# Attention and mixture of experts on one core: the last stores behind the first expert's gather, and four smaller moves beside it

## The chip, the cores and the metric

One core of a Trainium2 chip runs the whole kernel. The metric is the device time of one execution in microseconds. Three runs of the kernel before gave 411.78, 412.25 and 407.70 us; the median is 411.78. One more execution was profiled. The engines named here are TensorE (PE, with its weight loads PEld), VectorE (DVE), ScalarE (ACT), GpSimd (POOL) and SyncE (SP); SP and POOL hand transfers to the DMA engines.

## What is computed

```python
scores = scale * np.matmul(q, k.transpose(0, 1, 3, 2))          # 8 batches, 8 heads, 576 tokens, 64 wide
attn = softmax(np.where(masks, scores, -1e9))                   # heads 0-3 local (32 wide), 4-7 strided by 32
x = np.matmul(attn, v)  ->  (4608, 512)                          # tokens of batch b are rows 576*b ...
out = x.copy()
do_compute = x @ w_skip > 0
e_idx = np.argmax(xc @ w_gate, axis=1)                          # xc = x[do_compute]; one expert of 8 per token
for e in range(8):
    h = np.maximum(xc[mask_e] @ w1[e], 0.0)                     # 512 -> 1024
    y[mask_e] = gate_w[mask_e, None] * (h @ w2[e])              # 1024 -> 512
out[do_compute] = xc + y
```

All numbers are float32. A matmul with a weight is made of three, with each operand split into a rounded part and its remainder (xh and xl, w1h and w1l, w2h and w2l, hh and hl).

## The kernel before

**Attention** (to about 163 us of the profile). A unit is (b, pr): batch b, and pr 0 and 1 for the two parts of the local heads, 2 and 3 for those of the strided ones; 32 units run in turn (loop at L921). For each, qk (L195) makes the scores two units ahead, DVE adds the mask and takes the row maximum mx, POOL subtracts it (L234, into sm or frame; DVE takes part of it in batch 0), tex (L239) turns the result and takes exp, pv (L268) multiplies by V, and xpose (L328) turns the output x. A batch's x goes to DRAM with SP's stores (jobs_out, L313): kind 0 for the local half, 3 transfers, kind 1 for the strided half, 6 transfers in packets of 512 bytes.

**Routing.** score (L373), route1 (L390) and route2 (L439) find each token's expert and its slot; scat (L471) writes a row of the table in DRAM for 128 tokens at a time, an indirect DMA issued by POOL. Groups of one or two batches are routed together; the last three groups are batches 5, 6 and 7, with five scatters each.

**The first expert** ("e") is picked from the counts of batches 0 to 3, and 288 of its tokens, all from batches 0 to 5, are taken before the rest is known. In unit (7,1) POOL reads their table rows (rows, L638; tile tab, 96 partitions by 3), in unit (7,2) it gathers their x back from DRAM (gather, L690; tile xg, three indirect DMAs, L695). After the last unit, xturn (L706) transposes xg on TensorE (L715), ACT rounds it to xh (L717), DVE takes the remainder xl (L718). ffn1a (L752) makes the first two hidden blocks: sixteen matmuls with xh (L760), then eight with xl (L764); hout (L730) makes hh on ACT and hl on DVE. ffn1 (L737) makes hidden blocks 3 to 8, ffn2 the output.

**Weights** come in eight pieces of 512 KB per expert, w1 as pieces 1 to 4 and w2 as 5 to 8 (indices j = 0 to 7 in the code). wdma (L594) fetches a piece into one of three raw buffers, wcast (L605) rounds it on ACT, wrest (L615) subtracts on DVE and frees the buffer. For the first expert the lists CASTS, RESTS and FETCH (L43 to L45) say behind which unit a step stands; pieces 6 and 7 are made to wait for the gather (taken).

**The other experts.** TURN gives their order, by size. Behind the first expert's second matmuls come its overflow tokens ("l", 128 of them) and the experts' tokens r; their table rows are read by POOL and SP, and their gathers wait for all stores and scatters.

The order on each engine is that of the code: manual_schedule keeps it for the engines listed, and an engine runs its queue in that order, each instruction waiting for its semaphores. SP's transfers stand at the hand() calls of the loop.

## Time and profile before

| | us |
|---|---|
| median of three runs | 411.78 |
| profiled execution, its time | 412.99 |
| its span on the core | 411.2 |
| TensorE busy | 383.1 (93%) |
| DVE busy | 271.7 (66%) |
| POOL busy | 209.4 (51%) |
| ACT busy | 194.7 (47%) |
| granted clock, mean of the core | 0.981 |

The profiled execution's time is its span and 1.8 us around it. TensorE is busy nearly all of the span, so the time is read from the places where it waits and where its granted clock is below 1. A timeline row gives the start, the duration, the operation with its tiles, how many were merged, and in brackets the idle time before it with what ended it. A window gives busy times within a stretch.

### The profile page before, as it was taken

To read this page: it belongs to the slowest core of one execution; us is meant where nothing else is said; L and a number is where in the kernel's file an instruction comes from. 1 tells how busy PE (TensorE), PEld (TensorE's weight loads), DVE (VectorE), ACT (ScalarE), POOL (GpSimd) and SP (SyncE) were. 2 spreads that over 40 slices of the span, in tenths; PEclk is the share of its full clock that TensorE was granted. 3 is DMA by queue.
4 is the path that set the end of the run, shared out by engine and by line. 5 is a ranking of instruction groups with operands and counts; after the bars stand their busy time and mean duration, and the time that the engine had idled before them with its cause. 6 is when DMAs were issued, how large, how long until landed. Compare 5 with 4: busy or idle time off the path is not lost. (4 is left out here: it accounts for less than half of the span.)

```text
span 411.2 us, 12396 instructions
## 1 busy us (share of the span) xinstructions
PE 383.1 (93%) x4967; PEld 349.2 (85%) x4968; DVE 271.7 (66%) x526; ACT 194.7 (47%) x372; POOL 209.4 (51%) x296
## 2 busy tenths in 40 slices
PE   6889998989989977799999999999999999999993
PEld 3778887778767766689989999999999999998983
DVE  3767769656886886474268667756757767588640
ACT  1456554637362844152444364554444554555520
POOL 3353425772678686567017577383474473641101
PEclk9899999999998999699999999999999999999999
DMA  7999899999899846608439778697586587685801
GB/s 257 370 337 286 268 288 297 285 274 314 266 233 268 247 135 167 185 4 272 140 104 257 199 221 247 171 250 222 200 208 210 179 241 226 187 260 128 286 8 50
DMA packets 49554, 89.91 MB, mean 219 GB/s; under 512 B 8742, under 2 KB 25518, under 8 KB 49486
## 3 DMA queue, kind: packets, MB, share of 16 engines
q1 hardware_dynamic: 41261, 75.32, 61.3%
q0 software_dynamic: 8224, 13.70, 11.3%
q8 instruction: 41, 0.67, 0.7%
q14 instruction: 28, 0.22, 0.2%
HBM read 70.35 MB, written 15.30 MB: 208 GB/s over the span
## 5 line engine op out<-in xcount | busy, mean ns | idle before, releaser
L721 PE MATMUL S<-xh,w1h 128*128 128x324 f32 (+4 forms) x248 | 75.8, 305 | 0.8 <-DVE hl L734 0.8
L722 PE MATMUL S<-xl,w1h 128*128 128x324 f32 (+4 forms) x248 | 74.1, 299 | 0.0
L723 PE MATMUL S<-xh,w1l 128*128 128x324 f32 (+4 forms) x248 | 74.1, 299 | 0.0
L808 POOL DMA_INDIRECT out_dram<-ot,tab x23 | 27.1, 1176 | 85.6 <-DVE ot L802 51.3
L658 POOL DMA_DIRECT2D xq<-xg x96 | 52.6, 568 | 24.7 <-DVE xt L673 16.6
L617 DVE TENSOR_TENSOR w1l<-raw,w1h 128x1024 fp32r<-128x1024 f32 x32 | 39.0, 1227 | 27.1 <-ACT w1h L612 25.0
L733 ACT ACTIVATE hh<-S 128x324 fp32r<-128x324 f32 (+4 forms) x64 | 26.7, 418 | 52.3 <-PE S L723 42.9
L617 DVE TENSOR_TENSOR w2l<-raw,w2h 128x1024 fp32r<-128x1024 f32 x32 | 39.2, 1224 | 15.5 <-ACT w2h L612 15.4
L721 PEld LDWEIGHTS S<-xh,w1h 128*128 128x128 f32 x248 | 46.8, 189 | 1.2 <-DVE hl L734 1.1
L722 PEld LDWEIGHTS S<-xl,w1h 128*128 128x128 f32 x248 | 46.8, 189 | 0.1
L723 PEld LDWEIGHTS S<-xh,w1l 128*128 128x128 f32 x248 | 46.8, 189 | 0.0
L472 POOL DMA_INDIRECT table<-pay,rdi x38 | 38.8, 1021 | 10.3 <-issue 7.1
L234 POOL TENSOR_TENSOR sm<-sm,mx 128x384 f32<-128x384 f32 (+1 forms) x30 | 27.9, 941 | 31.0 <-PE T L254 13.9
L205 PE MATMUL S<-kt,qt 64*64 64x54 f32 (+1 forms) x1280 | 33.0, 241 | 9.8 <-DVE sm L223 3.5
L205 PEld LDWEIGHTS S<-kt,qt 64*64 64x64 f32 x1280 | 26.9, 139 | 16.0 <-issue 8.6
L734 DVE SCALAR_TENSOR_TENSOR hl<-S,hh 128x324 fp32r<-128x324 f32 (+4 forms) x64 | 29.3, 461 | 12.0 <-ACT hh L733 11.8
L612 ACT CAST w2h<-raw 128x1024 fp32r<-128x1024 f32 x32 | 33.4, 1043 | 5.5 <-DMA raw<-in_w_dram 5.5
L612 ACT CAST w1h<-raw 128x1024 fp32r<-128x1024 f32 x32 | 33.4, 1053 | 4.0 <-DMA raw<-in_w_dram 4.0
L234 POOL TENSOR_TENSOR frame<-sm,mx 128x324 f32<-128x324 f32 (+1 forms) x32 | 22.8, 725 | 18.5 <-DVE mx L229 18.4
L695 POOL DMA_INDIRECT xg<-out_dram,tab x23 | 26.3, 1145 | 11.3 <-issue 6.1
L262 ACT ACTIVATE ptl<-T 96x512 f32<-96x512 f32 (+1 forms) x40 | 19.5, 548 | 23.9 <-PE T L254 23.6
L311 DVE TENSOR_TENSOR x<-PV,rc 128x384 f32<-128x384 f32 (+1 forms) x64 | 29.5, 502 | 1.1
(181 smaller groups left out, 940.9 us busy)
## 6 DMA issues: line engine op xcount, KB each, us to landing
raw<-in_w_dram SPq DMA_DIRECT2D x64, 512.0 KB
vt<-in_vs_dram SPq DMA_DIRECT2D x16, 390.0 KB
qt<-in_qp_dram SPq DMA_DIRECT2D x16, 304.0 KB
kt<-in_kp_dram SPq DMA_DIRECT2D x16, 297.0 KB
kt<-in_kp_dram SPq DMA_DIRECT2D x14, 304.0 KB
vt<-in_vl_dram SPq DMA_DIRECT2D x16, 260.0 KB
out_dram<-x SPq DMA_DIRECT2D x16, 256.0 KB
qt<-in_qp_dram SPq DMA_DIRECT2D x14, 288.0 KB
```

The source lines that it names most:

```text
L205: mark[0] = T.matmul(s[HP * (i ^ j):HP * (i ^ j) + HP, j, (blk - b0) * win:(blk - b0 + 1) * win], lhsT=qt[p, j, blk * nq:blk * nq + HP], r ...
L234: (V if b == kind == 0 and j else G).tensor_tensor(e[:, j], sw[:, j], mx[:, j].unsqueeze(2).broadcast_to([128, b1 - b0, win]), op=ALU.subt ...
L311: V.tensor_tensor(outs[o], num, den, op=ALU.mult)
L472: i = G.indirect_dma_start(out=table, out_offset=bass.IndirectOffsetOnAxis(ap=di[:, t:t + 1], axis=0), in_=pay[:, t, :], in_offset=None, b ...
L612: A.copy(hi, raw)
L617: V.tensor_tensor(lo, raw, hi.bitcast(F32), op=ALU.subtract)
L658: G.dma_start(dst, src)
L721: T.matmul(p, lhsT=a[0], rhs=b[0], start=start, stop=False)
L722: T.matmul(p, lhsT=a[0], rhs=b[1], start=False, stop=False)
L723: T.matmul(p, lhsT=a[1], rhs=b[0], start=False, stop=stop)
L734: V.scalar_tensor_tensor(s["hl"][:, f, :C], p[:, :C], 0.0, s["hh"][:, f, :C].bitcast(F32), op0=ALU.max, op1=ALU.subtract)
L808: i = G.indirect_dma_start(out=out, in_=ot[:P], in_offset=None, bounds_check=NTOK - 1, oob_is_err=False, out_offset=bass.IndirectOffsetOnA ...
```

## The change

Five things move; what is computed stays.

- **SP.** The stores of batch 6's strided half and all of batch 7's, fifteen transfers, move behind the first expert's gather and wait for it, as pieces 5 and 6 do. The stores of batch 6's local half go out in the first two hands of unit (7,0). Piece 4 is fetched at the end of unit (7,0), and pieces 7 and 8 ahead of the reading of the next two experts' rows.
- **POOL.** In unit (7,0) the five scatters of batch 5 take turns with the subtractions; the gather is written in unit (7,1) right behind the row read. The five scatters of batch 6 are cut in three and two, the two behind the sums of the last route1.
- **DVE.** The remainders of pieces 1, 2 and 3 (wrest) move: the first to unit (7,0), the second to (7,1), the third into route2 between its reduction and its slots. The four operations of count move behind the last route1.
- **TensorE.** Nine of the twelve transposes of xg stand ahead of the last route1's five, not six.
- **The last ranks** (route2 of batch 7) stand behind the whole of ffn1a, not between its xh and xl matmuls.

On SP, around the end of attention: raw_2547, raw_2548 and raw_2549 are the three raw buffers; x_2591 and x_2773 are batch 6's halves, x_3005 (x_3009 in the change) and x_3136 (x_3133) batch 7's. Before:

```order
L182 DMA out_dram<-x_2591 128x2x256 x2
L182 DMA out_dram<-x_2591 64x256
L182 DMA out_dram<-x_2773 18x11x128 x2
L182 DMA out_dram<-x_2773 18x10x128
L598 ISA
L598 DMA raw_2547<-in_w_dram 128x1024
L182 DMA out_dram<-x_2773 18x11x128 x2
L182 DMA out_dram<-x_2773 18x10x128
L598 ISA
L598 DMA raw_2548<-in_w_dram 128x1024
L182 DMA out_dram<-x_3005 128x2x256 x2
```

and with the change:

```order
L182 DMA out_dram<-x_2591 128x2x256 x2
L182 DMA out_dram<-x_2591 64x256
L599 ISA
L599 DMA raw_2547<-in_w_dram 128x1024
L599 ISA
L599 DMA raw_2548<-in_w_dram 128x1024
L182 DMA out_dram<-x_2773 18x11x128 x2
L182 DMA out_dram<-x_2773 18x10x128
L182 DMA out_dram<-x_2773 18x11x128 x2
L182 DMA out_dram<-x_2773 18x10x128
L599 ISA
L599 DMA raw_2549<-in_w_dram 128x1024
```

Pieces 4 and 5 (raw_2547, raw_2548) stand ahead of the strided stores of batch 6; piece 5 carries the wait for the gather, and every store behind it stands behind that wait.

On POOL, units (7,0) and (7,1): table is the scatters' target, frame and sm the subtractions' results, tab the rows read, xg the gather. Before:

```order
L234 TENSOR_TENSOR sm_81<-sm_81,mx 128x480 x2
L472 DMA table<-pay_93,rdi 40960x4 x5
L234 TENSOR_TENSOR frame_84<-sm_82,mx 128x6x54 x2
L234 TENSOR_TENSOR frame_85<-sm_83,mx 128x5x54 x2
L640 ISA
L640 DMA tab<-table 96x12
L695 DMA xg_3126<-out_dram,tab 96x512 x3
```

and with the change:

```order
L234 TENSOR_TENSOR sm_81<-sm_81,mx 128x480 x2
L473 DMA table<-pay_93,rdi 40960x4 x2
L234 TENSOR_TENSOR frame_84<-sm_82,mx 128x6x54
L473 DMA table<-pay_93,rdi 40960x4
L234 TENSOR_TENSOR frame_84<-sm_82,mx 128x6x54
L473 DMA table<-pay_93,rdi 40960x4 x2
L234 TENSOR_TENSOR frame_85<-sm_83,mx 128x5x54 x2
L641 ISA
L641 DMA tab<-table 96x12
L696 DMA xg_3049<-out_dram,tab 96x512 x3
```

The same nine instructions stand ahead of the read of tab; the first two subtractions moved ahead of three and two of the scatters, and two follow the last scatter in place of four.

On DVE, from the last route1 (L422 to L425) to the first remainders of the hidden blocks: rdd, rds, rdi and pay are the last ranks and slots, pt, pr, fsel and isel the four operations of count. Before:

```order
L422 TENSOR_TENSOR rohb<-cs,rmw 128x40
L424 TENSOR_REDUCE rrs<-rohb 128x8
L425 TENSOR_TENSOR run_69<-run_70,rrs 128x8
L455 TENSOR_TENSOR rdd<-T,rohb 128x40
L457 TENSOR_REDUCE rds<-rdd 128x5
L459 TENSOR_TENSOR rdi<-rds,rmk 128x5
L460 RECIPROCAL pay_95<-rz 128x5
L734 SCALAR_TENSOR_TENSOR hl<-S,hh 128x288 x2
```

and with the change:

```order
L422 TENSOR_TENSOR rohb<-cs,rmw 128x40
L424 TENSOR_REDUCE rrs<-rohb 128x8
L425 TENSOR_TENSOR run_69<-run_70,rrs 128x8
L516 TENSOR_TENSOR pt_3361<-first,cnt_3263 1x8
L518 TENSOR_REDUCE pr_3363<-pt_3361 1x1
L519 SCALAR_TENSOR_TENSOR fsel<-pr_3363,fsel 1x1
L520 CAST isel<-fsel 1x1
L735 SCALAR_TENSOR_TENSOR hl<-S,hh 128x288 x2
L455 TENSOR_TENSOR rdd<-T,rohb 128x40
```

The two hl stand ahead of the last ranks instead of behind them, and the four operations of count, which stood ahead of the last batch's score copies, are now between route1 and hl.

```diff
--- before.py
+++ after.py
@@ -41,8 +41,8 @@
 PB = 3
 CB = 5
 CASTS = [(6, 3), (7, 0), (7, 1)]
-RESTS = [(7, 1), (7, 2), (7, 3)]
-FETCH = [(6, 0), (6, 1), (6, 3), (7, 2), (7, 3)]
+RESTS = [(7, 0), (7, 1)]
+FETCH = [(6, 0), (6, 1), (6, 3), (7, 0)]
 CE = (96, 3)
 
 CAPS = [(126, 3), (108, 3), (108, 3), (104, 3), (102, 3), (98, 3), (92, 3)]
@@ -177,11 +177,11 @@
             jobs.append((vt[0:LW, LV - 1].rearrange("p h c -> p (h c)"), vh[b]))
         return jobs
 
-    def issue(jobs, behind=None):
+    def issue(jobs, *behind):
         for dst, src in jobs:
             i = nc.sync.dma_start(dst, src).ins
-            if behind is not None:
-                tc.add_manual_dep(i, behind.name, SYNC, reason="a transfer is handed over beside its step")
+            for x in behind:
+                tc.add_manual_dep(i, x.name, SYNC, reason="a transfer is handed over beside or behind its step")
 
     pvp = psum.tile([128, 2, 512], F32, name="PV", tag="PV", bufs=1)
     v2 = [ap.tile([128, LV - 1, 4, 65], F32, name=f"v2{i}") for i in range(2)]
@@ -455,6 +455,7 @@
         V.tensor_tensor(dd, rkv, ohb, op=ALU.mult)
         ds_ = sp("rds", [128, nt])
         V.tensor_reduce(ds_, dd, axis=AX.X, op=ALU.add)
+        yield
         di = sp("rdi", [128, nt], I32)
         V.tensor_tensor(di, ds_, mk, op=ALU.add)
         V.reciprocal(pay[:, :, 2].bitcast(F32), zs)
@@ -930,6 +931,8 @@
             ob = jobs_out(units[n - 4][0], units[n - 4][1] // 2) if n > 3 else [[], []]
             steps = [vj[0:1], vj[1:], ob[0], qk_[0:1], qk_[1:2], qk_[2:3], qk_[3:4], ob[1]]
             steps = [[x for x in y if x is not None] for y in steps]
+            if b == NB - 1:
+                steps = [ob[0], ob[1]] if pr == 0 else []
         if n + LA >= len(units) and "h" not in pool:
             zctx.close()
             pool["h"] = ctx.enter_context(tc.tile_pool(name="hpool", bufs=1, side="right", reuse_waits="tile"))
@@ -965,8 +968,7 @@
         for x in front:
             next(x, 0)
         if b == CB + 2 and pr == 0:
-            while sc_:
-                scat(*sc_.pop(0))
+            scat(*sc_.pop(0))
         run(*rank, *late, *front)
         late = []
         if (b, pr) in RESTS:
@@ -995,8 +997,9 @@
         if n == 1:
             for g in range(len(GROUPS)):
                 payload(g)
-        if sc_ and n + 1 < len(units):
-            scat(*sc_.pop(0))
+        for _ in range(2 if b == CB + 2 and pr == 0 else 1):
+            if sc_ and n + 1 < len(units):
+                scat(*sc_.pop(0))
         if b == PB + 2 and pr == 3:
             e0 = nc.sync.value_load(isel[0:1, 0:1], min_val=0, max_val=NE - 1)
         if b == PB + 2 and pr == 3:
@@ -1009,23 +1012,28 @@
                 assert not sc_
             if pr == 1:
                 rows("e", s0, *CE, eng=G)
-            if pr == 2:
                 gather("e", "e", "e", last=(CB + 1) * S)
     pool_order.close()
     nr = len(GROUPS) - 1
     with tc.manual_schedule(engines={T.engine, A.engine, V.engine, G.engine}):
-        run(pv(*units[-1]), xpose(*units[-2]), route2(ranked, of=CB))
+        r2 = route2(ranked, of=CB)
+        run(pv(*units[-1]), xpose(*units[-2]), islice(r2, tiles(ranked) + 2))
+        wrest("e", 2)
+        run(r2)
+        for _ in range(3):
+            scat(*sc_.pop(0))
+        xe, r1 = xturn("e"), route1(nr)
+        run(xpose(*units[-1]), score(NB - 1), islice(xe, 9))
+        next(r1)
+        run(xe, r1)
+        count(CB)
         while sc_:
             scat(*sc_.pop(0))
-        count(CB)
-        run(xpose(*units[-1]), score(NB - 1), xturn("e", 0, 2))
-        r1 = route1(nr)
-        next(r1)
-        run(xturn("e", 2, 4), r1)
-    for kind in range(2):
-        for part in jobs_out(NB - 1, kind):
-            issue(part)
-    wdma("e", e0, 5, 6, st_["e"]["taken"])
+    with tc.manual_schedule(engines={nc.sync.engine}):
+        for kind in range(2):
+            wdma("e", e0, 4 + kind, 5 + kind, st_["e"]["taken"])
+            for part in jobs_out(NB - 2 + kind, 1 - kind) + jobs_out(NB - 1, 1) * kind:
+                issue(part, *st_["e"]["taken"])
     pctx.close()
     pctx = ExitStack()
     psum, bufs = pctx.enter_context(tc.tile_pool(name="psumT", bufs=1, space=PSUM, reuse_waits="tile")), {"S": 2, "T": 3, "PV": 2, "R": 1}
@@ -1036,22 +1044,23 @@
         x = nc.sync.value_load(order[0:1, n, r:r + 1], min_val=0, max_val=(NE - 1) * (1, ESTR)[n])
         (es, slots)[n][r] = x
 
-    with tc.manual_schedule(engines={T.engine, A.engine, V.engine, G.engine}):
-        run(islice(ga, 8), later(route2, nr), ga)
+    with tc.manual_schedule(engines={T.engine, A.engine, V.engine, G.engine, nc.sync.engine}):
+        run(ga, later(route2, nr))
         while sc_:
             scat(*sc_.pop(0))
         places = sort(NB - 1)
         g = ffn1("e", 2, 6)
         run(islice(g, 4))
         judge, rest = places()
+        wsplit("e", 3, 4)
+        wdma("e", e0, 6, 7)
+        run(islice(g, 4))
+        wsplit("e", 4, 5)
+        wdma("e", e0, 7, 8)
         for r in TURN[:2]:
             load(r, 1)
             assert SMALL[r] == CAPS[r]
             rows(r, slots[r], *CAPS[r])
-        wsplit("e", 3, 4)
-        wdma("e", e0, 6, 7, st_["e"]["taken"])
-        run(islice(g, 4))
-        wsplit("e", 4, 5)
         run(g)
         actx.close()
         pool["b"] = ctx.enter_context(tc.tile_pool(name="bpool", bufs=1, reuse_waits="tile"))
@@ -1069,7 +1078,6 @@
             load(key, 0)
         wdma(key, es[key], j, j + 1)
 
-    ahead(1)
     s0n = G.value_load(isel[0:1, 2:3], min_val=0, max_val=(NE - 1) * ESTR + CE[0] * CE[1])
     rows("l", s0n, CT, 1, eng=G)
     ahead(2)
```

## Rows read from the trace of the kernel before

**Rows 1.** Timeline, TensorE, 150 to 199: start, us, operation, count, [idle before <-releaser]
```profile
154.05 0.76 PE L254 MATMUL T<-cs,frame 128*118 128x128 f32 x5 [1.15 <-POOL frame L234]
...
154.74 0.47 PE L402 MATMUL T<-cs,s9s 9*128 9x9 f32 x5
...
164.06 0.36 PE L715 MATMUL T<-cs,xg 96*128 96x96 f32 x1
...
166.31 0.36 PE L715 MATMUL T<-cs,xg 96*128 96x96 f32 x1 [1.88 <-DMA xg<-out_dram,tab]
...
167.53 0.92 PE L715 MATMUL T<-cs,xg 96*128 96x96 f32 x4 [0.86 <-DMA xg<-out_dram,tab]
...
169.95 0.59 PE L760 MATMUL S<-xh,w1h 128*128 128x288 f32 x1
...
173.69 0.30 PE L760 MATMUL S<-xh,w1l 128*128 128x288 f32 x1
...
174.02 1.31 PE L764 MATMUL S<-xl,w1h 128*128 128x288 f32 x8
...
175.79 0.40 PE L721 MATMUL S<-xh,w1h 128*128 128x288 f32 x1 [0.44 <-DVE hl L734]
...
197.38 0.39 PE L715 MATMUL T<-cs,xg 128*128 128x128 f32 x2
```

**Rows 2.** Windows: us, busy (count) of PE, PEld, DVE, ACT, POOL; granted clock, DMA, GB/s
```profile
158.00:162.00 4.00, 2.26 (x56) 2.02 (x57) 3.04 (x9) 2.07 (x5) 3.26 (x5) 1.00 0.67 158
...
164.00:166.00 2.00, 0.42 (x7) 0.20 (x1) 1.28 (x5) 0.00 (x0) 1.61 (x2) 1.00 0.93 294
...
170.00:172.00 2.00, 2.00 (x10) 2.00 (x9) 1.62 (x6) 0.83 (x3) 0.06 (x1) 0.50 0.91 160
...
178.00:182.00 4.00, 3.65 (x28) 3.41 (x27) 3.75 (x9) 2.78 (x5) 3.27 (x4) 1.00 0.02 1
```

**Rows 3.** Timeline, POOL, 150 to 200
```profile
151.56 3.63 POOL L234 TENSOR_TENSOR frame<-sm,mx 128x324 f32<-128x324 f32 x4
...
157.84 1.04 POOL L695 DMA_INDIRECT xg<-out_dram,tab  x1 [1.53 <-DMA tab<-table]
...
160.47 0.96 POOL L695 DMA_INDIRECT xg<-out_dram,tab  x1 [0.32 <-issue]
...
175.47 1.06 POOL L472 DMA_INDIRECT table<-pay,rdi  x1 [2.04 <-DVE pay L460]
...
180.69 0.98 POOL L472 DMA_INDIRECT table<-pay,rdi  x1 [0.30 <-issue]
...
188.42 1.03 POOL L695 DMA_INDIRECT xg<-out_dram,tab  x1 [0.30 <-issue]
```

**Rows 4.** Issue to landing, us: gathers 157:162, scatters 175:183, gathers 190.6:192
```profile
DMA to landing us min/median/max: 7.0/7.0/7.0
...
DMA to landing us min/median/max: 2.9/2.9/2.9
...
DMA to landing us min/median/max: 7.2/7.2/7.2
```

**Rows 5.** Timeline, SP's queue, 150 to 182
```profile
159.50 0.66 SPq L598 DMA_DIRECT2D raw<-in_w_dram  x1
...
160.20 8.29 SPq L182 DMA_DIRECT2D out_dram<-x  x9
```

**Rows 6.** Timeline, DVE, 149 to 180
```profile
149.48 1.21 DVE L617 TENSOR_TENSOR w1l<-raw,w1h 128x1024 fp32r<-128x1024 f32 x1
...
163.93 0.14 DVE L519 CAST isel<-fsel 1x1 int32<-1x1 f32 x1
...
171.08 0.19 DVE L410 TENSOR_REDUCE rm<-T 128x5 f32<-128x40 f32 x1
...
172.70 0.17 DVE L425 TENSOR_TENSOR run<-run,rrs 128x8 bf16<-128x8 bf16 x1
...
175.28 0.99 DVE L734 SCALAR_TENSOR_TENSOR hl<-S,hh 128x288 fp32r<-128x288 f32 x2
```

## The prediction

> **What bounds the kernel now.** I read the timeline of TensorE first, for its waits, then the windows (busy time and granted clock), then the same minutes of POOL, SP and DVE. From 175.79 on TensorE stops only once more, for 0.35 us, before the tail; up to 154 it stops for little. What can be won lies between. At 164.06 it runs the first transpose of the first expert's tokens (tile xg, L715), then waits 1.88 us and 0.86 us for the rest of the gather [rows 1]. After those waits the granted clock is 0.50, the lower level of 1.2 GHz: it stood at 1.00 while TensorE was busy 2.26 of 4 us (158 to 162), and TensorE was busy only 0.42 of 2 us just before it fell [rows 2]. At that clock the sixteen L760 matmuls stand (173.69 - 169.95) / 15 = 0.249 us apart; 28 matmuls of the same size in 178 to 182 take 3.65 us, 0.130 each [rows 1, 2]. So this place costs twice: waits, then half speed.
>
> Why is the gather late? POOL issues its three parts at 157.84 (when the row table, tab, has landed) to 160.47, and each lands 7.0 us after its issue [rows 3, 4]; 160.47 + 7.0 = 167.5 is where the second wait ends. In those 7 us SP issues a weight piece of 512 KB at 159.50 and nine stores from 160.20 on [rows 5], and the DMA engines are 0.93 busy [rows 2]. Scatters issued in 175 to 183, with DMA at 0.02, land after 2.9 us [rows 4, 2].
>
> **The change, part by part.** I follow one mark: the start of the third hidden block, L721 at 175.79 [rows 1].
>
> *Stores behind the gather.* The order on POOL shows that the gather is not issued sooner: five scatters, four subtractions, the tab read, three gathers, as before; only the turns differ. What moves is SP: it now holds weight piece 5 and the last fifteen stores until the gather has landed. Piece 4 goes out at the end of unit (7,0), as soon as DVE has freed its buffer, long before the gather. So the gather has the DMA engines to itself, and the gain is its landing time alone. No row shows a gather in a quiet stretch. Bounds: 2.9 us, a scatter of 128 short rows in quiet, and 7.0 us, the same gather in traffic. I take the lower bound plus its data: 96 rows of 2 KB are 197 KB, 0.7 us at the 294 GB/s of 164 to 166 [rows 2], so 3.6 us, near the quiet end because the queue will be quiet. The third part then lands at 160.47 + 3.6 = 164.1, not 167.5.
>
> The Trainium skill ("DMA: Bandwidth & Descriptors", Anatomy of one DMA — SWDGE (gpsimd) path) gives about 2.0 us plus bytes at 436 GB/s, an estimate of 2.45 us here; no run here shows that, the 7.0 us of the trace is far from it, and by it the mark below would come 6.1 us sooner in place of 5.8.
>
> *From landing to mark, all at full clock.* Seven transposes at 0.15 (five took 0.76, [rows 1]) end at 165.1. The five L402 transposes take 0.47 to 165.6; the score copies that they need end on DVE by then in either order. The last three L715: 166.0. Then two chains run. TensorE: 16 x 0.130 = 2.1 and eight more in 1.31 [rows 1], to 169.4. Here lies the reason for ranking later: the rank matmuls now stand behind these eight. DVE: the last cast and subtraction of xg (some 0.5 us each, taken from the two hl of 0.99, which are as large) to 167.0; the routing chain, 171.08 to 172.87, 1.8 us; the four count operations on one partition now behind it, 0.14 us each (163.93) and as much again between them or less, 0.7 us in all; the first hl, 0.5 us [rows 6]. That is 170.0, later than TensorE, so DVE sets the mark: **175.79 - 170.0 = 5.8 us** sooner.
>
> *Subtractions in turns.* Each weight remainder is 1.21 us of DVE [rows 6]. The first moves ahead of the mask add of (7,3). That delays TensorE there by 1.21 us at most; it is covered by the 1.15 us that TensorE waited for frame [rows 1], and that wait goes because frame now passes three scatters of 1.3 us ((180.69 - 175.47) / 4, [rows 3]). The third leaves its place between two PV results for one behind the rank sums, worth 1.21 us at most. Neither counts: whether TensorE reaches L715 at 162.8 or 164.06, it has to wait until 164.1. Only a full 1.21 us late and uncovered would show, as 1.2 us. Price 0.
>
> *Scatters in turns.* The same nine instructions stand ahead of the tab read, but only two subtractions instead of four behind the last scatter, for whose landing the read waits. So the last scatter starts two subtractions later, some 1.8 us (four took 3.63, [rows 3]); at its quiet 2.9 us [rows 4] it lands about when the last subtraction ends, at twice that 2.9 us later. I take 0 and keep 2.9 for the range.
>
> *What is late next.* After the mark TensorE is the bound, and everything that it fetches must also come 5.8 us sooner. Two things may not. First, the expert gathers: the overflow tokens' part of 188.42 landed 7.2 us later, at 195.6, and TensorE used it at 197.38 [rows 3, 4, 1]; it will now ask at 191.6. Its chain on POOL starts with the last group's five scatters, 175.47 to 181.67 [rows 3]. They need the last ranks, ready some 3.5 us sooner, but two scatters of the group before (2.6 us) and a register load, which I put at 1 us, now stand between the last routing sums (about 169.5) and them: I get 173.2, 2.3 us sooner, so a landing at 193.3 if it still takes 7.2. That is a wait of up to 1.7 us. It may take less, because pieces 7 and 8 no longer travel beside it: at 5 us no wait is left. I take 0.8. Second, pieces 7 and 8 queue behind all the stores: one and a half batches of 1.18 MB and two pieces, 2.8 MB from 164.2 on; 10 us at 294 GB/s, 18 us at 158 [rows 2]. Landed 3.6 us later and split in 2.3 (cast and subtraction), they are there at 180 to 188; TensorE wants them at about 187. This lies inside the same 0 to 1.7 us.
>
> **Sum.** 5.8 - 0.8 = 5.0 us. The profiled execution took 412.99 us (span 411.2 and 1.8 around it): 408.0. The median of the three runs is 1.2 us lower, so for a median 411.78 - 5.0 = **406.8**.
>
> **Rivals.**
> 1. *The clock still falls.* TensorE still idles about 1.5 us before 164.1. For it: two waits of 1.88 and 0.86 us were enough. Against: 158 to 162 kept 1.00 with as little as 2.26 of 4 us busy [rows 2]. Price: L760 16 x 0.12 = 1.9 us and the transposes at 0.19 to 0.23 (four in 0.92, [rows 1]), 0.7 us; DVE is then no longer last, so the mark comes 3.4 us sooner, and the gathers have time. 408.4. The Trainium skill ("TensorE: Matmul & The Clock Gate", Part 1: The HAM clock gate) says that throttled is the default and activity releases it; the trace agrees in so far as 0.50 came behind the idle stretch and 1.00 came back while TensorE was working (174).
> 2. *The gather lands no sooner:* 7.0 us is its own price, not that of traffic. For it: the expert gathers took 7.2. Against: those too had weights beside them. Then the waits and the clock stay; 0.5 us from the new order of L402. 411.3.
> 3. *The wait is handed on in full* to the expert gathers, with 1.7 us and a little more for the rows fetched by SP: 3.8 us left, 408.0.
> 4. *Slower:* the place is SP behind the gather. With 2.8 MB of stores and pieces held back, pieces 7 and 8 come too late for the second matmuls. At 158 GB/s the stall is about 1 us; the gain is used up at about 122 GB/s (23 us of traffic), and at 100 GB/s (28 us) the kernel is 5 us slower, 416.8. Against: no stretch of [rows 2] with the stores in it is under 158.
>
> **How the numbers follow.** Forecast (gain 4.2 to 6.5) 0.48; clock falls 0.18; gather no sooner 0.12; wait handed on 0.12; slower 0.05; better than forecast, up to 8 us, 0.05. Range: from 411.0 (rival 2 at its upper end) to 402.5: the best gain is 403.8, and the three runs themselves spread from 407.7 to 412.25, so a median can lie another 1.3 lower. Given the forecast alone I expect 405 to 408. Over 1% (about what a measurement of this kernel can tell from no change) is 4.1 us: forecast and better make 0.53, rivals 1 to 3 make 0.42 within 1%, and slower 0.05.
>
> **What would show it.** Right: gather issues still near 157.8 to 160.5, landing in about 3.6 us; no half clock before the first hidden blocks; L721 6 us sooner, its wait on hl. Handed on: a wait at the overflow tokens' L715, or at the second matmuls' piece 7. Wrong: a landing of 7 us with only piece 4 ahead, or 0.50 again. The prediction fails most easily on the landing time, which no row measures in quiet, and on the 0.8 us.

## The result and the profile after

| | us |
|---|---|
| kernel before, median of 22 runs | 410.02 |
| changed kernel, median of 22 runs | 412.48 |
| ratio, with its 95% interval | 1.0057 [1.0035, 1.0079] |
| profiled execution after, its time | 412.04 |
| its span; mean granted clock | 410.3; 0.976 |
| predicted | 406.8 (402.5 to 411.0) |

The change made the kernel 0.6% slower, not 1.2% faster, and 412.5 lies outside the range. Later sessions showed that this answer belongs to one of two levels at which the same kernels run: in three sessions, the one of this table among them, the kernel before took 410 to 411 us (the lower level), in four 421 to 423 us (the upper level), and two chips met both. At the upper level the change gains 1.4%, in the one session that timed it there. All comparisons below are within a session or within a level. (The ratios leave out slow runs; where these are a third of the runs or more, for after_again, no_hold_d and lfirst_f, the median of all runs is given with them.)

TensorE's timeline after; the mark, the start of the third hidden block, is L722 now, and the tokens' transposes are L716:

```profile
160.44 1.08 PE L716 MATMUL T<-cs,xg 96*128 96x96 f32 x7 [0.51 <-DMA xg<-out_dram,tab]
...
166.50 0.40 PE L722 MATMUL S<-xh,w1h 128*128 128x288 f32 x1 [0.28 <-DVE hl L735]
...
193.27 0.70 PE L716 MATMUL T<-cs,xg 128*128 128x128 f32 x2 [4.97 <-DMA xg<-out_dram,tab]
...
200.94 0.51 PE L716 MATMUL S<-cs,xg 108*128 108x108 f32 x3
```

Up to the mark all goes as forecast: the third part of the gather (issued at 157.26, next fence) is there at 160.44, no half clock follows, and the mark stands at 166.50, waiting for hl. Before, it stood at 175.79 [rows 1]; some 3 us of that difference are an attention stage that ran earlier in this execution (POOL reads the row table, tab, for the first gather at 152.50, before at 155.72). Then TensorE stands still for 4.97 us ahead of the overflow tokens' transposes. The kernel before ran them at 197.38 without a wait [rows 1].

Windows after (columns as in [rows 2]):

```profile
162.00:166.00 4.00, 4.00 (x37) 3.88 (x37) 3.26 (x16) 1.04 (x3) 3.10 (x7) 1.00 0.61 198
...
186.00:190.00 4.00, 2.30 (x18) 2.06 (x16) 0.00 (x0) 0.40 (x1) 3.10 (x3) 1.00 0.97 271
190.00:194.00 4.00, 0.73 (x4) 0.74 (x5) 0.00 (x0) 0.21 (x1) 2.15 (x3) 0.81 0.75 190
194.00:198.00 4.00, 4.00 (x19) 4.00 (x18) 0.93 (x4) 1.40 (x6) 0.00 (x0) 0.50 0.12 44
198.00:202.00 4.00, 4.00 (x30) 4.00 (x30) 0.00 (x0) 0.80 (x2) 0.00 (x0) 0.84 0.00 0
```

The clock falls behind that wait as it fell before behind the first gather: 0.50 in 194 to 198 and 0.84 in 198 to 202. The place has moved; the pattern, a wait and then half speed, has not.

POOL, and SP's queue, after:

```profile
157.26 0.96 POOL L696 DMA_INDIRECT xg<-out_dram,tab  x1 [0.30 <-issue]
...
174.16 0.98 POOL L473 DMA_INDIRECT table<-pay,rdi  x1 [0.30 <-issue]
...
178.43 0.61 POOL L641 DMA_DIRECT2D tab<-table  x1 [1.89 <-DMA table<-pay,rdi]
182.87 1.75 POOL L696 DMA_INDIRECT xg<-out_dram,tab  x1 [3.83 <-DMA tab<-table]
...
186.29 1.03 POOL L696 DMA_INDIRECT xg<-out_dram,tab  x1 [0.30 <-issue]
```

```profile
161.03 4.35 SPq L182 DMA_DIRECT2D out_dram<-x  x6
...
166.25 7.99 SPq L182 DMA_DIRECT2D out_dram<-x  x9
175.31 1.00 SPq L599 DMA_DIRECT2D raw<-in_w_dram  x2
177.96 1.77 SPq L641 DMA_DIRECT2D tab<-table  x2
```

In the kernel before, POOL's row read and first expert gather were:

```profile
183.46 0.61 POOL L640 DMA_DIRECT2D tab<-table  x1 [0.40 <-issue]
185.64 1.11 POOL L695 DMA_INDIRECT xg<-out_dram,tab  x1 [1.57 <-DMA tab<-table]
```

The last scatters are 6.5 us sooner than in [rows 3], but the row read behind them (L641) starts only at 178.43, 5.0 us sooner than before, and the first expert gather at 182.87, 2.8 us sooner, less than the attention stage was ahead. So the lead is lost at two landings: the scatters' took 3.3 us (175.14 to 178.43; before 1.8 at most, 181.67 to 183.46), and from POOL's row read to the gather it took 4.4 us (before 2.2). The overflow tokens' part is third, at 186.29. In SP's queue the held stores go out until 174.2, then pieces 7 and 8, and only then the two row reads; the first gather starts 4.9 us after the first of them.

### The profile page after: what moved, and what is told of

Read it like the earlier page. It is cut to its first block, busy times and chain, and to the rows that moved or that the text cites. A ratio compares the mean times of both kernels' runs of the same rounds, so it can differ in the third digit from the quotient of the medians.

```text
span 410.3 us, 12399 instructions
## 1 busy us (share of the span) xinstructions
PE 382.7 (93%) x4967; PEld 349.4 (85%) x4968; DVE 271.3 (66%) x526; ACT 194.6 (47%) x372; POOL 210.3 (51%) x296
## 5 line engine op out<-in xcount | busy, mean ns | idle before, releaser
L722 PE MATMUL S<-xh,w1h 128*128 128x324 f32 (+4 forms) x248 | 75.9, 306 | 0.7 <-DVE hl L735 0.7
L722 PEld LDWEIGHTS S<-xh,w1h 128*128 128x128 f32 x248 | 46.9, 189 | 1.1 <-DVE hl L735 1.0
L205 PE MATMUL S<-kt,qt 64*64 64x54 f32 (+1 forms) x1280 | 31.8, 241 | 6.3 <-DMA kt<-in_kp_dram 2.8
L735 DVE SCALAR_TENSOR_TENSOR hl<-S,hh 128x324 fp32r<-128x324 f32 (+4 forms) x64 | 29.4, 462 | 11.1 <-ACT hh L734 10.9
```

The source lines that it names most:

```text
L205: mark[0] = T.matmul(s[HP * (i ^ j):HP * (i ^ j) + HP, j, (blk - b0) * win:(blk - b0 + 1) * win], lhsT=qt[p, j, blk * nq:blk * nq + HP], r ...
L722: T.matmul(p, lhsT=a[0], rhs=b[0], start=start, stop=False)
L735: V.scalar_tensor_tensor(s["hl"][:, f, :C], p[:, :C], 0.0, s["hh"][:, f, :C].bitcast(F32), op0=ALU.max, op1=ALU.subtract)
```

## Where the lead goes: both kernels in one session

**after_again, before_again.** The two kernels unchanged, for traces on one chip at one time.

> The changed kernel itself once more, beside the kernel before on the same chip. The runs so far show that chips differ (the kernel before 410.0 us on one, 422.9 us on another, where kernels with one edit to the changed kernel were 1.0 to 1.5% faster than it). If the loss of 0.6% belongs to the change, the ratio is 1.003 to 1.008 again, with a wait of 4 to 5 us at the overflow tokens. If the chip's own state decides how much of the lead is handed back, the ratio may fall below 1.00, and the wait at the overflow tokens is shorter.

> The kernel before, for its trace on the same chip as the three beside it. If its stage from 155 to 200 us is as in the trace read ahead of the prediction (third part of the gather landed 7.0 us after its issue, clock 0.50 in 170 to 172, no wait at the overflow tokens), the comparison on this chip is the same as there; if the landings differ by over 1 us, the terms of the sum depend on the chip.

Measured: 0.9996 [0.9955, 1.0037]; the medians of all runs, 412.0 against 410.65, make 1.003. The kernel before, TensorE, POOL and one window:

```profile
172.48 0.40 PE L721 MATMUL S<-xh,w1h 128*128 128x288 f32 x1 [0.44 <-DVE hl L734]
...
194.06 0.39 PE L715 MATMUL T<-cs,xg 128*128 128x128 f32 x2
...
199.01 0.51 PE L715 MATMUL S<-cs,xg 108*128 108x108 f32 x3
...
177.38 0.99 POOL L472 DMA_INDIRECT table<-pay,rdi  x1 [0.30 <-issue]
...
180.16 0.60 POOL L640 DMA_DIRECT2D tab<-table  x1 [0.40 <-issue]
182.16 1.16 POOL L695 DMA_INDIRECT xg<-out_dram,tab  x1 [1.40 <-DMA tab<-table]
...
184.99 1.03 POOL L695 DMA_INDIRECT xg<-out_dram,tab  x1 [0.30 <-issue]
...
176.00:180.00 4.00, 3.64 (x28) 3.41 (x27) 3.25 (x6) 1.97 (x4) 3.36 (x3) 1.00 0.02 1
```

and the changed kernel:

```profile
166.82 0.40 PE L722 MATMUL S<-xh,w1h 128*128 128x288 f32 x1 [0.27 <-DVE hl L735]
...
195.24 0.70 PE L716 MATMUL T<-cs,xg 128*128 128x128 f32 x2 [6.63 <-DMA xg<-out_dram,tab]
...
202.14 0.51 PE L716 MATMUL S<-cs,xg 108*128 108x108 f32 x3
...
174.46 0.98 POOL L473 DMA_INDIRECT table<-pay,rdi  x1 [0.30 <-issue]
...
180.28 0.61 POOL L641 DMA_DIRECT2D tab<-table  x1 [3.43 <-DMA table<-pay,rdi]
182.26 1.80 POOL L696 DMA_INDIRECT xg<-out_dram,tab  x1 [1.37 <-DMA tab<-table]
...
185.72 1.03 POOL L696 DMA_INDIRECT xg<-out_dram,tab  x1 [0.30 <-issue]
...
176.00:180.00 4.00, 4.00 (x31) 3.86 (x30) 1.53 (x3) 1.05 (x3) 0.84 (x1) 1.00 0.85 252
```

At the mark the change is 172.48 - 166.82 = 5.66 us ahead. At the overflow tokens it is 1.2 us behind, and at the next expert's transposes 202.14 - 199.01 = 3.1 us behind. TensorE waits 6.63 us; from these transposes to the next expert's it takes 6.90 us where the kernel before takes 4.95, so the fall of the clock costs 2.0 us more (2.7 in the first pair of traces: 200.94 - 193.27 against 202.32 - 197.38). The account closes: 5.66 - 6.63 - 2.0 is 3.0 us lost, 3.1 are read at the next expert. (The two traces end 2.9 us apart, the medians 1.4, so this pair shows more of the loss than the medians do.)

POOL shows why. The last scatter ends at 175.44 instead of 178.37, 2.9 us sooner. The row read, which waits for its landing, starts at 180.28 instead of 180.16: the landing took 4.8 us, with the DMA engines 0.85 busy in 176 to 180, where it took 1.8 us at most at 0.02. So the gathers start at the same time in both kernels (182.26 and 182.16), and TensorE, 5.66 us ahead at the mark, finds nothing when it asks. On top of that the part then lands later: 195.24, where the kernel before used it at 194.06 without a wait.

**The upper level: after_c and before_d.**

> The changed kernel once more, as the measure for the three beside it on the same chip. Its wait at the overflow tokens was 4.97 and 6.63 us in two traces; expected 4 to 7 us again, and a ratio to the kernel before of 0.996 to 1.008. On a chip like the one where the kernel before took 422.9 us, the wait may be under 1 us instead, and the ratio under 1.

> The kernel before, for its trace beside these. If it takes about 422 us here, its trace tells where the 12 us come from that it takes more than at 410: the stretch of the last attention units and the gather (150 to 180 us) with the clock at half for 8 to 12 us is expected, since the changed kernel's trace in that state shows the clock at 0.52 to 0.91 from 148 to 176. If it takes 410 us: as before, third part of the gather landed 7 us behind its issue, clock 0.50 for about 6 us.

Measured: after_c 417.05 against 422.3, ratio 0.9864 [0.9834, 0.9894]; before_d, in another session, 420.4. Of before_d, ScalarE and a window; of after_c, TensorE and a window:

```profile
175.86 0.40 ACT L717 CAST xh<-T 128x288 fp32r<-128x288 f32 x1 [5.44 <-remote]
...
164.00:168.00 4.00, 3.53 (x50) 2.92 (x49) 2.82 (x8) 2.33 (x5) 0.39 (x2) 0.50 0.37 98
```

```profile
176.41 0.40 PE L722 MATMUL S<-xh,w1h 128*128 128x288 f32 x1 [0.27 <-issue]
...
202.40 0.70 PE L716 MATMUL T<-cs,xg 128*128 128x128 f32 x2 [3.91 <-DMA xg<-out_dram,tab]
...
164.00:168.00 4.00, 4.00 (x49) 2.83 (x48) 2.28 (x9) 1.44 (x4) 1.10 (x1) 0.52 0.63 165
```

The kernel before reaches the mark at 182.52 here, 10.0 us later than in before_again, and the changed kernel at 176.41, 9.6 us later than in after_again: the clock is down in several stretches from 148 on, and in before_d ScalarE and VectorE have waits of up to 5.7 us that the profile puts down to "remote", which the traces at the lower level do not have. The lead at the mark is 6.1 us in this pair, but that near agreement is no support: nine other traces at this level, of kernels that hold the same stores and are the changed kernel up to the mark, reach it between 170.49 (lfirst_rows_first_d) and 178.62 (lfirst_e). The wait at the overflow tokens is 3.91 us, 2.7 us less than in after_again. Of the scatters' lead, 3.1 us (185.33 against 188.41 at the end of the last), 1.6 us are left when the gathers start (190.52 against 192.14), where at the lower level nothing was. This pair of traces is only 1.2 us apart at the end (418.4 and 417.2 span); after_c's profiled run is 1.9 us above its median, so the 5.2 us between the medians are not all to be found in it. Why less is given back at this level is not settled by one pair, and neither is what makes the level.

## Experiments on the hold of the stores

Each is an edit of the changed kernel.

**no hold (x6_no_hold, no_hold_d).** The stores do not wait for the gather:

```diff
-            wdma("e", e0, 4 + kind, 5 + kind, st_["e"]["taken"])
             for part in jobs_out(NB - 2 + kind, 1 - kind) + jobs_out(NB - 1, 1) * kind:
-                issue(part, *st_["e"]["taken"])
+                issue(part)
+        for kind in range(2):
+            wdma("e", e0, 4 + kind, 5 + kind, st_["e"]["taken"])
```

> The 15 last stores no longer wait for the first expert's gather: SyncE hands them over as they become ready, and pieces 5 and 6 behind them, still waiting for the gather. All else is as in the changed kernel. In the changed kernel the start of the third hidden block comes at 166.50 us, and later TensorE waits 4.97 us for the overflow tokens' gather (row at 193.27), with the clock at 0.50 from 194 to 198. Theory 1 (the held stores hand the wait on): the stores, done at 174 in the changed kernel, are over before 166; the gather's third part lands some 3.5 us later (as in the kernel before, 7.0 us from its issue), so the mark comes about 3.5 us later, near 170; the rows of the next two experts land some 2 us after they are asked for instead of 3.5 to 4.9, and the wait at the overflow tokens is under 2 us, partly because TensorE itself arrives 3.5 us later. End: 408 to 411. Theory 2 (GpSimd's own chain and a 7 us gather are late in any case, whatever the stores do): the overflow tokens land near 193 again, TensorE arrives near 192, wait near 1.5 us and end within 1 us of the changed kernel's 412. The two part at the landing of the overflow tokens: under 191 or near 193.

> The last stores not held behind the gather. Where the kernel before took 422.9 us this was 1.002 of it, against 0.986 for the changed kernel: the hold was worth 1.6% there, with the clock at half for most of 164 to 176 without it. With the kernel before at 410 us: the start of the third hidden block 3 to 5 us later than 166.8, the wait at the overflow tokens 0 to 3 us, and a ratio of 0.997 to 1.005, so that the hold is worth nothing to 2 us there.

Measured, both at the upper level: 1.0021 [0.998, 1.0061] and 0.9922 [0.9875, 0.9969] (the medians of all runs of no_hold_d, 421.2 against 420.57, make 1.002). In the same sessions the kernels with the hold and one or two other edits (below) gave 0.985 to 0.990. TensorE of no_hold_d:

```profile
167.02 0.43 PE L716 MATMUL T<-cs,xg 96*128 96x96 f32 x1 [2.15 <-DMA xg<-out_dram,tab]
168.95 1.40 PE L716 MATMUL T<-cs,xg 96*128 96x96 f32 x7 [1.50 <-DMA xg<-out_dram,tab]
...
193.94 0.61 PE L722 MATMUL S<-hh,w2h 128*128 128x288 f32 x1 [5.86 <-DVE hl L735]
```

The waits for the gather are back, and the mark comes at 177.51, where the kernel with the gathers' order alone, in the same session, had it at 172.03. So between these two kernels, timed side by side, the hold is worth 5.5 us at the mark, near what the prediction said. The other run is less clear: the mark of x6_no_hold is at 177.21, where three kernels with the hold, timed beside it, have it at 171.78, 172.70 and 174.79, and its trace shows no wait for the gather, but the clock at 0.50 from 162 to 174. Not all of the loss in time is this: piece 8, now last in the queue, is 3.3 us late for its cast, and TensorE waits 5.86 us for the second matmuls (5.49 in x6_no_hold). The two shares are not separated.

**early, both.** Piece 5 and six stores go out in units (7,1) and (7,2), where the DMA engines are idle; only piece 6 and nine stores wait for the gather:

```diff
-FETCH = [(6, 0), (6, 1), (6, 3), (7, 0)]
+FETCH = [(6, 0), (6, 1), (6, 3), (7, 0), (7, 1)]
-                steps = [ob[0], ob[1]] if pr == 0 else []
+                steps = [ob[0], ob[1]]
...
```

(behind the gather, the loop that is not shown here keeps piece 6 and batch 7's stores), and in "both" the overflow tokens are gathered first as well:

```diff
-    gather("l", "b", "h")
-    for i in range(2):
-        gather(TURN[i], "b", "eh"[i])
-    G.memset(ring("b", "xq", 1, 4 * CMAX), 0.0)
+    with tc.manual_schedule(engines={G.engine}):
+        G.memset(ring("b", "xq", 1, 4 * CMAX), 0.0)
+        gather("l", "b", "h")
+        for i in range(2):
+            gather(TURN[i], "b", "eh"[i])
```

> The first half of the kernel with both edits alone: piece 5 and batch 6's strided stores in the units (7,1) and (7,2), the gathers in the changed kernel's order (overflow tokens third). Theory 1: the wait at the overflow tokens falls from 4.97 us to 0 to 2.5 us, the time to 3 to 5 us under the changed kernel; what is left to the kernel with both edits is the price of the third place. If the six stores, now beside the first gather, slow it (landing over 4 us after issue instead of 3.2), the start of the third hidden block comes later by as much and the gain is lost there.

> Piece 5 and batch 6's strided stores are handed over in the attention units (7,1) and (7,2), while the DMA engines are nearly idle (share 0.02 from 150 to 154 in the changed kernel), so that only piece 6 and batch 7's stores wait for the gather; and GpSimd gathers the overflow tokens first. Theory 1 (the held stores hand the wait on, through rows that land 4 to 5 us after they are asked for, and the overflow tokens' third place among the gathers makes it worse): the last store is done 4 to 6 us sooner than 173.97, the rows land about 2 us after they are asked for, the overflow tokens land before TensorE asks, no wait there and no half clock, some 6 us under the changed kernel and 1 to 1.5% under the kernel before. If the wait comes from GpSimd's chain of scatters: 0 to 2 us under the changed kernel.

Measured, in the session of after_again: early 1.0124 [1.007, 1.0179], 415.55 us; both 1.0020 [0.9979, 1.0061], 411.48. Both of my expectations failed: neither kernel is faster than the changed one by what was expected, and the third hidden block comes later, though not through a slower gather. Early, SP, POOL, TensorE and a window; then TensorE of early and of both at the overflow tokens:

```profile
148.12 4.14 SPq L182 DMA_DIRECT2D out_dram<-x  x6
...
154.21 0.59 POOL L641 DMA_DIRECT2D tab<-table  x1 [3.17 <-issue]
157.54 1.32 POOL L696 DMA_INDIRECT xg<-out_dram,tab  x1 [2.75 <-DMA tab<-table]
...
162.00:166.00 4.00, 2.90 (x17) 2.41 (x17) 2.81 (x11) 1.19 (x3) 2.81 (x5) 0.50 0.49 111
```

```profile
198.18 0.51 PE L716 MATMUL T<-cs,xg 128*128 128x128 f32 x2 [4.17 <-DMA xg<-out_dram,tab]
```

```profile
195.96 0.51 PE L716 MATMUL T<-cs,xg 128*128 128x128 f32 x2 [0.47 <-DMA xg<-out_dram,tab]
```

The idle stretch was not free. The first gather's row read waits for scatters too; the last of them ended at 149.77, and with six stores on the way, piece 5 just ahead of them, the read starts at 154.21, 4.4 us later (the profile names no releaser for this wait). In after_again it starts 2.0 us behind its last scatter (150.82, 152.84). The gather follows at 157.54, 2.6 us later than there, TensorE waits for it 2.35, 0.84 and 0.80 us, and the clock is 0.50 in 162 to 170. The mark comes at 172.09. It looks like the chain behind the mark: scatters, row read, gather, delayed by what travels beside the scatters. That the traffic is the reason here is argued from the order in time; no run separates it.

Between early and both only the order of the gathers differs: the wait at the overflow tokens is 4.17 us in one and 0.47 in the other, and the medians are 4.1 us apart.

## Experiments on the wait at the overflow tokens

**lfirst** (lfirst, lfirst_c, lfirst_d, lfirst_e, lfirst_f): the second diff above alone. In the changed kernel two parts of the next expert stand ahead.

> GpSimd gathers the overflow tokens first, ahead of the next two experts' first parts; nothing else is changed. In the changed kernel that gather is third: 186.29 for its issue, against 182.87 of the first, and TensorE waits for it 4.97 us (row at 193.27), then runs 194 to 198 at the clock 0.50. If the order of the gathers is what makes the wait: issue no later than 182.9, and as it needs no rows fetched by SyncE (only its own table row, read at 178.43) perhaps at 180.5 to 181; landing 187.5 to 190, the wait 0 to 2 us, no half clock, end 404 to 409. If instead the gather's latency of 7 us under traffic is set by the pieces' transfers that end near 188, it lands near 190 to 191 whatever its place, and the wait is 2 to 3 us with the clock still falling: end near 410. A wait that moves to the next expert (first gather two places later, near 185) would show as idle time ahead of that expert's transposes.

> The same kernel as in the run before this one, for the state in which the kernel before takes about 410 us, which four sessions with it have not met. There: theory 1 (the third place among the gathers makes most of the wait of 5 to 6.6 us) 0 to 3 us of wait and a ratio of 0.985 to 0.996; rival (the landing is late in any place) over 3 us and 0.997 to 1.006. With the kernel before at 420 us or more: no wait again and 0.979 to 0.987.

Measured at the upper level, four sessions: 0.9853 [0.9797, 0.991], 0.9856 [0.9827, 0.9884], 0.9866 [0.9817, 0.9915], 0.9791 [0.9732, 0.985], no wait in any of the four traces; beside the changed kernel (after_c) 415.9 against 417.05 us. At the lower level, lfirst_f: 0.9891 [0.9836, 0.9947] from three of its six runs; the median of all six is 409.73 against 410.13, 0.999. So at this level a gain over the kernel before is not shown. TensorE and POOL of lfirst_f, from an execution of 411.49 us:

```profile
169.86 0.40 PE L722 MATMUL S<-xh,w1h 128*128 128x288 f32 x1 [0.27 <-DVE hl L735]
...
194.83 0.70 PE L716 MATMUL T<-cs,xg 128*128 128x128 f32 x2 [2.95 <-DMA xg<-out_dram,tab]
...
186.63 1.07 POOL L696 DMA_INDIRECT xg<-out_dram,tab  x1 [2.13 <-DMA tab<-table]
```

The wait is 2.95 us, not 4.97 or 6.63, but not gone: the part is issued first, at 186.63, and still takes 8.2 us to land, with the DMA engines 0.93 to 1.07 busy from 188 to 194. Measured from the mark it lands 25.0 us later, in the first trace of the change 26.8 and in after_again 28.4. By the bounds set beforehand, the wait lies at the edge of the theory's range and the ratio of all six runs in the rival's: both hold a share.

**Rows ahead of pieces 7 and 8** (x5_rows_first; with lfirst: lfirst_rows_first, lfirst_rows_first_d).

```diff
-        wdma("e", e0, 6, 7)
-        run(islice(g, 4))
-        wsplit("e", 4, 5)
-        wdma("e", e0, 7, 8)
         for r in TURN[:2]:
             ...
+        wdma("e", e0, 6, 7)
+        run(islice(g, 4))
+        wsplit("e", 4, 5)
+        wdma("e", e0, 7, 8)
```

> Pieces 7 and 8 of the first expert (0.5 MB each, at 175.31 in the changed kernel) go back behind the rows of the next two experts in SyncE's queue, as in the kernel before. Theory 1 (whole cause is the hold on the stores, done at 173.97): the rows are still asked for behind the stores, and the pieces overlap them or not; first expert gather comes less than 1 us sooner than 182.87, the wait at the overflow tokens stays over 4 us, end 411 to 412.5. Theory 3 (1 MB of pieces ahead of the rows in the same queue is what makes the rows take 3.5 to 4.9 us): the rows land some 2 us after they are asked for, the first expert gather starts at 180 to 181, the overflow tokens land near 191, the wait falls to some 2.5 us, end near 409; pieces 7 and 8 themselves then come 2 to 3 us later, which would show as a wait of the cast ahead of the second block's matmuls.

> Overflow tokens gathered first, and pieces 7 and 8 behind the rows in SyncE's queue. In the changed kernel the last scatter ends at 175.4 and the table's row is read only at 178.4 to 180.3, 3 to 5 us later, where the kernel before needs 1.8 us; the two pieces (1 MB) are on the way in that time. If they are what holds the scatters' landings: the row is read 2 us behind the last scatter, the gathers start 2 to 3 us sooner than 182.3, and there is no wait at the overflow tokens; if pieces 7 and 8 are not late for their casts, 5 to 8 us faster than the changed kernel. If the stores are (done at 173.1 to 174.0): no more than the kernel with the gathers' order alone.

Measured: 0.9863 [0.9801, 0.9924]; with lfirst 0.9892 [0.985, 0.9935] and 0.9866 [0.9805, 0.9926]; all at the upper level. POOL and SP of lfirst_d, and of lfirst_rows_first_d in the same session:

```profile
180.44 1.34 POOL L473 DMA_INDIRECT table<-pay,rdi  x1 [0.30 <-issue]
...
186.64 0.60 POOL L641 DMA_DIRECT2D tab<-table  x1 [3.46 <-DMA table<-pay,rdi]
...
178.01 3.31 SPq L599 DMA_DIRECT2D raw<-in_w_dram  x2
```

```profile
178.01 0.98 POOL L473 DMA_INDIRECT table<-pay,rdi  x1 [0.31 <-issue]
180.79 0.61 POOL L641 DMA_DIRECT2D tab<-table  x1 [1.79 <-DMA table<-pay,rdi]
...
180.25 2.10 SPq L641 DMA_DIRECT2D tab<-table  x2
182.63 7.88 SPq L599 DMA_DIRECT2D raw<-in_w_dram  x5
```

With the pieces ahead the row is read 186.64 - 181.78 = 4.9 us behind the last scatter, with the rows ahead 180.79 - 178.99 = 1.8 us, and 1.8 us in the two other kernels with the rows ahead too. With the pieces ahead it is about 3 us or more in every trace but one. So, at the level where it was tried, pieces 7 and 8, and not the stores, are what the scatters' landing waits for; x6_no_hold and no_hold_d, whose stores are through by then, say the same with 5.4 and 5.7 us. The exception is lfirst: 1.8 us (184.19 to 186.00) with the first piece handed over at 180.79 and the second by 184.9. There next to no bytes moved from 184.2 to 185.4, just behind the last scatter, so what counts is the traffic at that moment and not the place in the queue alone. The time does not show any of this at the upper level: with lfirst no wait is left to take away, and the later pieces cost waits of the casts (5.1 us in lfirst_rows_first, of which TensorE sees 1.0). Theory 3's time is therefore not tested, and at the lower level the edit was not tried.

**lfirst_l_late and warm.** The transposes of "l" one block of second matmuls later (`if db == 3` for `db == 2`), with lfirst; and twenty matmuls on constants ahead of them, without it.

> Overflow tokens gathered first, and on TensorE their transposes stand behind the last quarter of the first expert's second product instead of ahead of it: 12 matmuls of 0.13 us at the full clock, 1.6 us of work put in front of the wait. If a rest of the wait is left with the gathers' order alone, it falls by up to 1.6 us and the time with it; if none is left, this is the same as that kernel within 0.5 us.

> Twenty matmuls of 512 columns on constants stand on TensorE ahead of the overflow tokens' transposes, where it waits 4.97 us in the changed kernel; their result is used by nothing. They take 20 times some 0.21 us, 4.3 us, inside the wait. This prices the fall of the clock apart from the wait. If the fall costs what the stretch shows (194 to 198 at 0.50, 198 to 202 at 0.84: 0.50 of 4 us and 0.16 of 4 us are 2.6 us of TensorE's full-speed time), the wait stays and the end comes some 2 to 3 us sooner, 409 to 410. If the stretch behind the wait is bound by other work (softmax on ScalarE and VectorE), the end moves by less than 0.5 us though the clock stays at 1.00.

Measured: 0.9858 [0.983, 0.9886], with lfirst alone 0.9856 beside it: no wait, nothing to hide. Warm: 0.9895 [0.9827, 0.9963], inconclusive. It fell into the upper level. Its twenty matmuls took 4.3 us from 198.38, 7.2 us after the overflow tokens' part was issued (191.22), and no wait is left behind them; whether they hid one is not shown, and so the run does not price the clock.

## Why the prediction was wrong, point by point

- **The gather in quiet: right.** 3.6 us was taken between 2.9 and 7.0; the traces give 3.2 (157.26 to 160.44) and 3.1 (157.59 to 160.71 in after_again). The estimate by the Trainium skill ("DMA: Bandwidth & Descriptors", Anatomy of one DMA — SWDGE (gpsimd) path), 2.45 us, is too low here; the measurement decides. Rivals 1 and 2 fall in both traces of the change at the level of the result: the clock stays at 1.00 and the landing is short. (Rival 1 is not excluded for every execution: lfirst_f, the same up to the mark and at the same level, has the clock at 0.54 in 164 to 166.)
- **The mark: right.** 5.8 us forecast, set by DVE's hl; 5.66 us in the pair from one session, with hl as the releaser. The subtractions and scatters in turns at price 0 fit that: from the first of the five scatters to the row read it takes 10.6 us in both traces of the change, 10.9 and 11.0 before. The agreement to 0.1 us is partly luck: in that pair the gather's third part is issued 0.8 us later than before (157.59, 156.79), and its landing falls from 7.7 to 3.1 us, more than the forecast 7.0 to 3.6.
- **"What is late next": wrong.** This step failed: the wait for the expert gathers, 0.8 us taken, 1.7 us at most; 4.97 and 6.63 us measured, and 2.0 to 2.7 us of lowered clock behind them, for which the step had no term. Two parts of it were off. The scatters are 2.9 us sooner (2.3 forecast; the 1 us for a register load had no row behind it and does not show, since the scatters follow each other at the usual 0.30 us). But I let the whole 2.3 us pass on to the gathers, as if the landings between them kept their quiet time. The scatters' landing takes 4.8 us in place of 1.8, with pieces 7 and 8, which the change puts ahead of the rows, on the way (moving them shows it, at the upper level), and the whole lead of the chain is gone; in the first trace 3.3 us, and the rows behind it take 4.4 in place of 2.2. And I let the part land 7.2 us after its issue or less, "because pieces 7 and 8 no longer travel beside it". The 7.2 was not its own: [rows 4] has it from gathers issued at 190.6 to 192, and no trace gives the landing of the one at 188.42. It took 7.0 us in the first trace and 9.5 in after_again (185.72 to 195.24), where the next expert's pieces and the other gathers keep the DMA engines 0.95 to 1.07 busy from 184 to 194. In after_again the two make 5.3 of the 6.63 us: an issue 3.0 us later than the step puts it (184.99 - 2.3 is 182.7), and a landing 2.3 us longer. The part was third among the gathers before as well, and the step took that as given; putting it first was worth 4.1 us between early and both.
- **Pieces 7 and 8 for the second matmuls: right.** No wait there in either trace of the change at the lower level; rival 4 did not happen.
- **Rival 3 came true**, the wait handed on in full, but it was priced at 1.7 us and a bit more (3.8 us left of the gain); the wait and the clock together took all of it, and more.
- **What stays open:** why the upper level keeps a gain of 1.4%. The sum of 5.0 us is near the 5.2 us between the medians there, but for a reason that it did not contain, so it is no support for it.

**A better version, as far as shown:** the gathers' order alone, lfirst. Against the kernel before it is 0.979 to 0.987 at the upper level, in four sessions; at the lower it is level with it by the median of all six runs (0.999). Against the changed kernel it is 1.1 us faster in one session at the upper level, where the intervals overlap, and 409.7 against 412.0 and 412.5 us at the lower, in different sessions.

## What to carry to other kernels

When a stage is brought forward, follow the next chain of small dependent transfers (scatter, row read, gather) to its end, and ask at each landing which bulk transfer will be on the way at the new time; a landing price from a quiet stretch does not move with the instruction. Put the part that is needed first at the head of its queue. Weight pieces that have slack may go behind the few rows that have none: that shortened the landing here, but no run shows a gain in time from it. And time a change at more than one level of the machine before its sign is believed: here the change made +0.6% at one and -1.4% at the other.

## What the runs showed of the hardware

- A scatter's landing, read from the end of the last scatter's issue to the row read that waits for it: 1.8 us with the pieces behind the rows (three traces), and 3.0 to 5.7 us with weight pieces on the way (13 traces; 3.0 in lfirst_e, 3.3 in the first trace of after, 4.8 in after_again, 4.9 in lfirst_d, 5.2 in lfirst_f, 5.7 in no_hold_d). One trace with the pieces ahead, lfirst, has 1.8 us, with next to no bytes moving just behind its last scatter.
- An indirect gather of 96 rows in quiet landed 3.1 to 3.2 us after its issue; one of 128 rows took 7.0 to 9.5 us with the DMA engines mostly at 0.75 to 1.07 (six traces in which TensorE waited for it).
- The kernel before took 410 to 411 us in some sessions and 421 to 423 us in others, and two chips met both. In after_c, at the upper level, the granted clock was 0.52 to 0.91 in most stretches from 148 to 176 us, where after_again had 1.00, and in most traces of that level engines other than TensorE showed waits put down to "remote". No run here shows the cause.
